# Moving the preparation of the next batch to other steps in a two-stage DFT and gated feed-forward kernel

## The chip, the cores and the metric

One core of a Trainium2 chip. The time is device time in microseconds of one execution, the median of repeated runs; smaller is better. The engines named below are TensorE (PE), VectorE (DVE), ScalarE (ACT), GpSimd (POOL) and SyncE (SP), which here only issues DMAs. Each engine works through its own instructions in the order in which the program lists them.

## The reference

For x of shape 8 x 3008 x 256 (batch, sequence, channel) the real part of a two-dimensional Fourier transform is taken over sequence and channel, and each of the 24064 resulting rows goes through a feed-forward block with the gate h cos h:

```python
X = np.fft.fft(x, axis=1)
X = np.fft.fft(X, axis=2)
a = X.real.astype(np.float32)            # 8 x 3008 x 256
h = a.reshape(-1, 256) @ w_in            # 24064 x 2048
g = h * np.cos(h)
out = (g @ w_out).astype(np.float32)     # 24064 x 256
```

## The kernel before

The channel transform is folded into w_in once at the start (WC and WS, line 351). The sequence transform of length 3008 = 47 x 64 is done per batch in two stages on PE. For x of a batch:

- `load_x` (line 139) brings one of four pieces p into a tile xp (four buffers): six DMAs for piece 0, four for the others, all on SP.
- `fold` (line 210) makes sums and differences of channel halves into xf (one buffer). In batches after the first that is one POOL operation for each of e = 0 and 1 (line 218); e = 1 adds a small ACT copy of two channels (line 225).
- `first_half` (line 231) multiplies a chunk c of xf by a 94-row DFT matrix into a PSUM tile pz (lines 241 to 251) and ACT copies it out (line 260). In batches after the first pz has the tag "fft", which has one buffer.
- `store_z` and `load_z` (lines 266, 278) pass the result through DRAM to change its layout, by SP DMAs.
- `second_half` (line 290) does the second stage of one group g of output rows: four matmuls into a PSUM tile pb, tag "fft" too (line 297), an ACT copy into pq (line 313), and two SP DMAs, one behind the other, that spread one row of pq over 128 partitions as nb (lines 319, 320).

The feed-forward part is a hand-written software pipeline. A batch has six groups (width 225 for group 0, else 256), each with eight steps of 256 hidden units, 48 steps in a batch and 384 in all. The main loop runs over t (line 740). A step `cur` at time t does `mm1(cur, 0)`, PE matmuls with WC into H; `act_e`, which copies twice H to ew (line 464); `mm1(cur, 1)`, matmuls with WS into the same H, which must wait until ew has been read; `dve_h` (line 469), the second side of the symmetric pair; and two ACT roundings (line 484). The gate follows over the next two values of t: `dve_frac` (488), `act_sin` (494), `dve_g` (498), `dve_s` (509 to 518). `mm2` of the step three earlier (line 545) accumulates seven products into M. `seed` (line 429) has ACT write the initial value of the next step's H from nb.

After the last step of a group, ACT copies M out (`take_m`, line 566), POOL combines (`combine_m`, lines 584 to 594; this runs in the steps with t mod 8 = 2 to 4), and `store_out` (line 634) transposes half of the result on DVE (line 637) into ob, then issues the output DMAs on SP (line 647), eight for each half of an ordinary group.

`transform(b)` (line 330) lists, by step of the batch before, the calls that prepare batch b: loads, folds, first stage, intermediate store and load, second stage. The main loop calls what is listed for a step at the end of that step, after `store_out` (line 786) and after the opening's own calls (line 790). The order in the program is the order of each engine's queue: what is called later stands behind what was called before on SP, POOL, ACT, DVE and PE alike.

Of the kernel before, what the change touches and what calls it, by code (L numbers as in the profile page):

```python
# [26 lines left out]
NG = 6  # L27
LAG = 3
# [64 lines left out]
def _runs(g, sg):  # L93


    runs = []
    for j, n, c in _cols(g):
        a, k = c, 0
        if sg:
            a, j = 256 - c - n, (N2 - j) % N2  # L100
            if j == 0:
                a, k, n = a + 1, 33, 31
        runs.append((a // 32, j, k, n))
    return runs
# [3 lines left out]
def kernel(  # L108
# [8 lines left out]
    NB = x.shape[0]  # L117
# [205 lines left out]
    def spread_nb():  # L323
        pq, nb = ready[0, 0]
        T = _width(0)
        pn = psum("pn", "M")
        nc.tensor.matmul(pn[:, 0:T], lhsT=ones, rhs=pq[0:1, T : 2 * T], start=True, stop=True)
        nc.scalar.copy(out=nb[:, 0:T], in_=pn[:, 0:T])

    def transform(b):  # L330
        todo = {}

        def at(o, *call):
            todo.setdefault(o, []).append(call)

        for p in range(4):
            at(8 * p + (0 if p else 3), load_x, b, p)
            for c, o, f in ((2 * p, 6, 8), (2 * p + 1, 9, 13)):
                at(8 * p + o, fold, b, c, 0)
                at(8 * p + o, fold, b, c, 1)  # L340
                at(8 * p + f, first_half, b, c)
                at(8 * p + f + 1, store_z, b, c)
        at(23, load_z, b, 0)
        at(39, load_z, b, 1)
        for g in range(NG):
            at(42 + g, second_half, b, g)
        return todo

    def fold_weights(e, n, tag="M"):
        W = WS if e else WC
        pw = psum("pw", tag)
        for i in range(2):
            nc.tensor.matmul(  # L355
                pw,
                lhsT=CS[i][:, 128 * e : 128 * e + 128],
                rhs=wr[n // 2][i][:, 512 * (n % 2) : 512 * (n % 2) + 512],
                start=(i == 0),
                stop=(i == 1),  # L360
            )
        nc.scalar.copy(out=W[:, 512 * n : 512 * n + 512], in_=pw)
# [74 lines left out]
    def seed_first(s):  # L437
        for u in range(2):
            nc.tensor.matmul(
                s.H[:, u * s.T : u * s.T + s.T],  # L440
                lhsT=wrow[:, 128 * u : 128 * u + 128],
                rhs=s.pq[0:1, s.T : 2 * s.T],
                start=False,
                stop=True,
                skip_group_check=True,
            )

    def mm1(s, e):
        T = s.T
        W = WS if e else WC  # L450
        for u in range(2):
            f = 2 * s.fp + u
            nc.tensor.matmul(  # L453
                s.H[:, u * T : u * T + T],
                lhsT=W[:, 128 * f : 128 * f + 128],
                rhs=s.pq[:, e * T : e * T + T],
                start=False,
                stop=True,
                skip_group_check=True,
            )  # L460

    def act_e(s):
        s.ew = spool.tile([128, 512], FP, tag="ew", bufs=2, name="ew")
        nc.scalar.mul(out=s.ew[:, 0 : 2 * s.T], in_=s.H[:, 0 : 2 * s.T], mul=2.0)  # L464
# [21 lines left out]
    def dve_frac(s, sg):  # L486
        r, h = side(s, sg)
        nc.vector.scalar_tensor_tensor(  # L488
            out=r, in0=r, scalar=-BIG, in1=h, op0=ALU.add, op1=ALU.subtract
        )  # L490
# [5 lines left out]
    def dve_g(s, sg):  # L496
        r, h = side(s, sg)
        nc.vector.scalar_tensor_tensor(  # L498
            out=r, in0=h, scalar=-0.25, in1=r, op0=ALU.add, op1=ALU.mult
        )  # L500
# [57 lines left out]
    def take_m(s, part):  # L558
        T = s.T
        key = (s.b, s.grp)  # L560
        if part == 0:
            mrs[key] = spool.tile([128, 7 * 256], FP, tag="mr", bufs=1, name="mr")
        mv = mrs[key].rearrange("p (m t) -> p m t", m=7)[:, :, 0:T]
        for k in (2, 3) if part else (0, 1):
            n = 1 if k == 3 else 2
            nc.scalar.mul(
                out=mv[:, 2 * k : 2 * k + n],
                in_=acc[key][k].rearrange("p (m t) -> p m t", m=2)[:, 0:n, 0:T],
                mul=TWO_PI,
            )  # L570
# [26 lines left out]
    def combine_last(s):  # L597
        key = (s.b, s.grp)
        M5, M3 = acc[key][2], acc[key][3]
        mv = mrs.pop(key).rearrange("p (m t) -> p m t", m=7)  # L600
        outs[key] = spool.tile([128, 7 * 256], FP, tag="cb", bufs=1, name="cb")
        cv = outs[key].rearrange("p (m t) -> p m t", m=7)
        tt, stt = nc.vector.tensor_tensor, nc.vector.scalar_tensor_tensor
        more = dict(op0=ALU.mult, op1=ALU.add)
        tt(out=cv[:, 0], in0=mv[:, 0], in1=mv[:, 1], op=ALU.add)
        stt(out=cv[:, 4], in0=M5[:, 256:512], scalar=-TWO_PI, in1=mv[:, 0], **more)
        stt(out=cv[:, 6], in0=M5[:, 0:256], scalar=TWO_PI, in1=cv[:, 4], **more)
        stt(out=cv[:, 1], in0=M3[:, 0:256], scalar=TWO_PI, in1=cv[:, 6], **more)
        store_last(s, 0)
        tt(out=cv[:, 5], in0=cv[:, 4], in1=mv[:, 3], op=ALU.add)  # L610
        tt(out=cv[:, 2], in0=cv[:, 5], in1=mv[:, 2], op=ALU.add)
        stt(out=cv[:, 3], in0=M5[:, 0:256], scalar=TWO_PI, in1=cv[:, 5], **more)
        store_last(s, 1)
# [20 lines left out]
    def store_out(s, sg):  # L634
        ob = spool.tile([128, 512], FP, tag="ob", bufs=2, name="ob")
        ov = ob.rearrange("p (t c) -> p t c", c=64)
        nc.vector.transpose(
            out=ov.rearrange("p t (c j) -> p j t c", j=2),
            in_=outs[s.b, s.grp][:, 512 * sg : 512 * sg + 512],
        )  # L640
        for t0, j, k, n in _runs(s.grp, sg):
            to = out_r[s.b, j].rearrange("k (q c) -> q k c", c=64)
            for i in range(0, n, 32):
                m = min(32, n - i)
                src, dst = ov[:, t0 + i // 32], to[:, k + i : k + i + m]
                if m == 32:
                    nc.sync.dma_start(out=dst, in_=src)  # L647
                    continue
                for q in range(4):
                    nc.sync.dma_start(out=dst[q], in_=src[32 * q : 32 * q + m])  # L650
# [70 lines left out]
    for b in range(NB):  # L721
        for g in range(NG):
            for fp in range(8):
                s = Step()
                s.b, s.grp, s.fp, s.T = b, g, fp, _width(g)
                steps.append(s)
    per = NG * 8
    n = len(steps)

    def step(t, last=None):  # L730
        s = steps[t] if 0 <= t < n else None
        return s if s is not None and (last is None or s.fp == 7) else None
# [7 lines left out]
    for t in range(n + LAG + 1):  # L740
        cur, prev, old, done = step(t), step(t - 1), step(t - 2), step(t - LAG)
        if cur:
            if t % per == 0:
                todo = transform(cur.b + 1) if cur.b + 1 < NB else {}
            mm1(cur, 0)
            if t == 0:
                seed_first(cur)
            act_e(cur)
            if t == 0:
                spread_nb()  # L750
                fold_weights(1, 3)
        if t - LAG - 1 == n - 1:
            combine_last(steps[n - 1])
            break
        if step(t - LAG - 1, True):
            take_m(step(t - LAG - 1), 1)
            combine_m(step(t - LAG - 1))
        if done:
            mm2(done, 0)
        if old:  # L760
            dve_g(old, 0)
            dve_g(old, 1)
        if step(t + 1):
            seed(step(t + 1))
        if prev:
            dve_frac(prev, 0)
        if old:
            dve_s(old, 0)
        if prev:
            dve_frac(prev, 1)  # L770
            act_sin(prev)
        if old:
            dve_s(old, 1)
        if step(t - LAG, True):
            take_m(done, 0)
        if cur:
            mm1(cur, 1)
        if done:
            mm2(done, 1)
        if cur:  # L780
            dve_h(cur)
            act_round(cur, 0)
            act_round(cur, 1)
        if old:
            dve_s(old, 2)
        if step(t - LAG - 2, True):
            store_out(step(t - LAG - 2), 0)
        if step(t - LAG - 3, True):
            store_out(step(t - LAG - 3), 1)
        for call in opening.pop(t, ()):  # L790
            call[0](*call[1:])
        for call in todo.pop(t % per, ()):
            call[0](*call[1:])


# [28 lines left out]
```

## Time and profile before

| what | us |
|---|---|
| median of 3 runs (1974.46 to 1974.85) | 1974.66 |
| span of the profiled execution | 1973.1 |
| first step of the main loop starts | 38.4 |
| batch 0, first step to first step of batch 1 | 247.1 |
| each of batches 1 to 6 | 241.1 |
| batch 7, first step to end of span | 241.0 |
| PE / DVE / ACT / POOL busy | 1948.9 / 1854.4 / 1482.7 / 465.1 |
| POOL waiting in `fold` for PE to release xf (line 218 on line 251) | 547.9 |
| SP waiting for the DVE before an output DMA (line 647) | 841.0 |

The span is that of one execution, from its first to its last instruction. A row of the timeline gives a start in us from the start of the span, a length, the engine and line, the operation with its output and inputs, and how many like instructions it merges; a bracket at its end gives idle time of the engine just before and what ended it. A row of busy time by stretch gives the stretch, its length, busy us and number of instructions of PE, weight loads, DVE, ACT and POOL, the granted TensorE clock, the DMA share and GB/s. Rows of neighbouring matmuls overlap, since they are pipelined; the distance from start to start is their cost. The letter q behind an engine's name is its sequencer, here the issue of DMAs.

### The profile page before, as it was taken

Reading aid. Unit: us, or ns where it says so; the run is one execution under the profiler, and the core shown is the slowest. Engines: PE = TensorE matmul, PEld = TensorE weight load, DVE = VectorE, ACT = ScalarE, POOL = GpSimd, SP = SyncE. Lnnn points to the kernel's source line nnn. Section 1 sums busy time; section 2 is a strip of 40 time slices with the busy share of each in tenths; the row PEclk is TensorE's granted clock in tenths of the full one; section 3 lists DMA queues with packets and bytes.
Section 4 is the critical chain, followed back from the end, with each engine's and each line's share of the span. In section 5 each row is a group of like instructions: output and inputs, shape, how many; then the busy total and the mean of one; then the engine's idle time right before and its main releaser. Section 6 shows DMA issues by size and latency. Waiting matters only on the chain.

```text
span 1973.1 us, 28657 instructions
## 1 busy us (share of the span) xinstructions
PE 1948.9 (99%) x9360; PEld 1702.4 (86%) x9360; DVE 1854.4 (94%) x3209; ACT 1482.7 (75%) x2687; POOL 465.1 (24%) x428
## 2 busy tenths in 40 slices
PE   8999999999999999999999999999999999999998
PEld 4888899888988889888898888988889888898887
DVE  2999989999899998999989999999999999899998
ACT  3777777777777777777877777777777777778775
POOL 1123113221133212223222322123311233112111
PEclk9999999999999999999999999999999999999999
DMA  8413221131212212122122301223022220200000
GB/s 194 100 41 62 41 43 31 40 59 35 43 33 46 51 36 43 38 59 38 34 41 51 63 20 37 45 53 55 19 42 53 43 51 21 47 21 10 19 15 22
DMA packets 176682, 88.63 MB, mean 45 GB/s; under 512 B 103303, under 2 KB 173622, under 8 KB 174902
## 3 DMA queue, kind: packets, MB, share of 16 engines
q1 hardware_dynamic: 176374, 86.68, 21.4%
q8 instruction: 75, 1.23, 0.3%
q14 instruction: 73, 0.60, 0.1%
q10 hardware_dynamic: 160, 0.13, 0.0%
HBM read 49.50 MB, written 37.27 MB: 44 GB/s over the span
## 4 chain that ended last, share of the span: by engine, by line
PE 91%; DVE 5%; DMA 2%; ACT 1%; issue 1%; SPq 0%; DVEq 0%; POOL 0%; ACTq 0%; POOLq 0%
PE M L545 53%; PE H L453 31%; PE pz L244 3%; PE pb L297 2%; DVE r L498 1%; DMA xp<-in_x_dram 1%; DVE S L516 1%; DVE S L509 1%; DVE S L518 1%; DVE h L469 1%; DVE r L488 1%; ACT r L484 0%; PE pw L355 0%; DMA out_dram<-ob 0%; SPq L647 0%
## 5 line engine op out<-in xcount | busy, mean ns | idle before, releaser
L494 ACT ACTIVATE r<-r 128x1024 f32<-128x1024 f32 (+1 forms) x384 | 398.5, 1038 | 303.6 <-DVE r L488 302.7
L545 PE MATMUL M<-S,VX 128*128 128x256 f32 (+1 forms) x2304 | 612.3, 375 | 0.0
L545 PEld LDWEIGHTS M<-S,VX 128*128 128x128 f32 x2304 | 437.8, 190 | 49.9
L453 PE MATMUL H<-pq,WS 128*128 128x256 f32 (+1 forms) x1536 | 390.2, 376 | 11.5 <-ACT ew L464 11.2
L453 PE MATMUL H<-pq,WC 128*128 128x256 f32 (+1 forms) x1536 | 393.9, 379 | 0.5 <-ACT H L429 0.5
L545 PE MATMUL M<-r,w 128*128 128x256 f32 (+1 forms) x1536 | 387.7, 375 | 0.0
L429 ACT ACTIVATE H<-nb,wn 128x256 f32<-128x256 f32 (+1 forms) x766 | 362.9, 474 | 18.0 <-DVE r L498 5.6
L469 DVE TENSOR_TENSOR h<-ew,H 128x512 f32<-128x512 f32 (+1 forms) x384 | 256.8, 669 | 92.5 <-PE H L453 86.5
L453 PEld LDWEIGHTS H<-pq,WS 128*128 128x128 f32 x1536 | 289.3, 190 | 53.9 <-ACT ew L464 20.0
L545 PEld LDWEIGHTS M<-r,w 128*128 128x128 f32 x1536 | 300.7, 197 | 27.0
L488 DVE SCALAR_TENSOR_TENSOR r<-r,h 128x512 f32<-128x512 f32 (+1 forms) x384 | 309.5, 806 | 0.0
L453 PEld LDWEIGHTS H<-pq,WC 128*128 128x128 f32 x1536 | 283.2, 190 | 28.9 <-ACT H L429 0.8
L218 POOL TENSOR_TENSOR xf<-xp 94x508 f32<-94x508 f32 x112 | 165.4, 1497 | 566.0 <-PE pz L251 547.9
L509 DVE TENSOR_TENSOR S<-r 128x512 f32<-128x512 f32 (+1 forms) x384 | 290.2, 756 | 0.1
L498 DVE SCALAR_TENSOR_TENSOR r<-h,r 128x512 f32<-128x512 f32 (+1 forms) x384 | 272.6, 710 | 0.0
L484 ACT ACTIVATE r<-H 128x512 f32<-128x512 f32 (+1 forms) x384 | 222.9, 580 | 55.7 <-DVE h L469 52.7
L464 ACT ACTIVATE ew<-H 128x512 f32<-128x512 f32 (+1 forms) x384 | 225.4, 587 | 50.3 <-PE H L453 43.8
L488 DVE SCALAR_TENSOR_TENSOR r<-r,H 128x512 f32<-128x512 f32 (+1 forms) x384 | 255.1, 664 | 0.0
L498 DVE SCALAR_TENSOR_TENSOR r<-H,r 128x512 f32<-128x512 f32 (+1 forms) x384 | 254.0, 661 | 0.3 <-ACT r L494 0.3
L484 ACT ACTIVATE r<-h 128x512 f32<-128x512 f32 (+1 forms) x384 | 236.2, 615 | 0.0
L545 PE MATMUL M<-S,w 128*128 128x256 f32 (+1 forms) x768 | 225.2, 375 | 0.0
L545 PE MATMUL M<-r,VX 128*128 128x256 f32 (+1 forms) x768 | 225.1, 375 | 0.0
(72 smaller groups left out, 1498.4 us busy)
## 6 DMA issues: line engine op xcount, KB each, us to landing
out_dram<-ob SPq DMA_DIRECT2D x728, 32.0 KB
xp<-in_x_dram SPq DMA_DIRECT2D x56, 256.0 KB
zd<-zs SPq DMA_DIRECT2D x112, 96.0 KB
z<-zd SPq DMA_DIRECT2D x28, 384.0 KB
xp<-in_x_dram SPq DMA_DIRECT2D x56, 120.0 KB
nb<-nd SPq DMA_DIRECT2D x40, 128.0 KB
wr<-in_moe_w_in_dram SPq DMA_DIRECT2D x8, 256.0 KB
w<-in_moe_w_out_dram SPq DMA_DIRECT2D x4, 512.0 KB
```

Of the source, the lines that this page charges most:

```text
L218: (nc.gpsimd if b else nc.vector).tensor_tensor(out=fv[:, e, :, 1:128], in0=xv[:, :, 1:128], in1=xv[:, :, 255:128:-1], op=ALU.subtract if ...
L244: nc.tensor.matmul(pz[rows, a:512], lhsT=w, rhs=fv[:, e, a:512], start=True, stop=True)
L429: nc.scalar.activation(out=s.H[:, u * T : u * T + T], in_=s.nb[:, 0:T], func=AF.Copy, bias=0.25, scale=wn[:, f : f + 1],)
L453: nc.tensor.matmul(s.H[:, u * T : u * T + T], lhsT=W[:, 128 * f : 128 * f + 128], rhs=s.pq[:, e * T : e * T + T], start=False, stop=True, ...
L464: nc.scalar.mul(out=s.ew[:, 0 : 2 * s.T], in_=s.H[:, 0 : 2 * s.T], mul=2.0)
L469: nc.vector.tensor_tensor(out=s.h[:, 0 : 2 * T].rearrange("p (u t) -> p u t", u=2)[:, :, ::-1], in0=s.ew[:, 0 : 2 * T].rearrange("p (u t) ...
L484: nc.scalar.activation(out=r, in_=h, func=AF.Copy, bias=BIG, scale=1.0)
L488: nc.vector.scalar_tensor_tensor(out=r, in0=r, scalar=-BIG, in1=h, op0=ALU.add, op1=ALU.subtract)
L494: nc.scalar.activation(out=r, in_=r, func=AF.Sin, bias=0.0, scale=SIN_SCALE)
L498: nc.vector.scalar_tensor_tensor(out=r, in0=h, scalar=-0.25, in1=r, op0=ALU.add, op1=ALU.mult)
L509: nc.vector.tensor_tensor(out=sv[:, 0:2], in0=gv[:, 2:3].to_broadcast([128, 2, T]), in1=gv[:, 0:4:3], op=ALU.subtract,)
L545: nc.tensor.matmul(acc[key][m // 2][:, 256 * (m % 2) : 256 * (m % 2) + T], lhsT=w, rhs=a, start=first, stop=s.fp == 7, skip_group_check=True,)
```

## The change

The dictionary of preparing calls is now one for the whole run, keyed by the absolute step, and filled before the main loop for batches 1 to 7, so that a call can be put into a step beyond the 48 of the batch before. Step numbers of the calls change, and the two `store_out` calls of a group come one step later.

```diff
+    todo = {}
+    per = NG * 8
+
     def transform(b):
-        todo = {}
-
         def at(o, *call):
-            todo.setdefault(o, []).append(call)
+            todo.setdefault(per * (b - 1) + o, []).append(call)
 
         for p in range(4):
-            at(8 * p + (0 if p else 3), load_x, b, p)
-            for c, o, f in ((2 * p, 6, 8), (2 * p + 1, 9, 13)):
+            at(8 * p + (1 if p else 5), load_x, b, p)
+            for c, o, f in ((2 * p, 7, 9), (2 * p + 1, 9, 15)):
                 at(8 * p + o, fold, b, c, 0)
                 at(8 * p + o, fold, b, c, 1)
                 at(8 * p + f, first_half, b, c)
                 at(8 * p + f + 1, store_z, b, c)
-        at(23, load_z, b, 0)
-        at(39, load_z, b, 1)
-        for g in range(NG):
-            at(42 + g, second_half, b, g)
-        return todo
+        at(25, load_z, b, 0)
+        at(41, load_z, b, 1)
+        for g, o in enumerate((44, 46, 49, 51, 54, 57)):
+            at(o, second_half, b, g)
...
     n = len(steps)
+    for b in range(1, NB):
+        transform(b)
...
-            if t % per == 0:
-                todo = transform(cur.b + 1) if cur.b + 1 < NB else {}
...
-        if step(t - LAG - 2, True):
-            store_out(step(t - LAG - 2), 0)
         if step(t - LAG - 3, True):
-            store_out(step(t - LAG - 3), 1)
+            store_out(step(t - LAG - 3), 0)
+        if step(t - LAG - 4, True):
+            store_out(step(t - LAG - 4), 1)
         for call in opening.pop(t, ()):
             call[0](*call[1:])
-        for call in todo.pop(t % per, ()):
+        for call in todo.pop(t, ()):
             call[0](*call[1:])
```

By step of the batch, before and after:

| call | before | after |
|---|---|---|
| load of x, piece 0 / piece p | 3 / 8p | 5 / 8p + 1 |
| fold of chunks 2p and 2p + 1 | 8p + 6, 8p + 9 | 8p + 7, 8p + 9 |
| first stage of chunks 2p and 2p + 1 | 8p + 8, 8p + 13 | 8p + 9, 8p + 15 |
| loads of the intermediate result | 23, 39 | 25, 41 |
| second stage of groups 0 to 5 | 42 to 47 | 44, 46, and 1, 3, 6, 9 of the next batch |
| transposes and output DMAs, t mod 8 | 4, 5 | 5, 6 |

## The prediction, made before the changed kernel was run

> **What bounds the kernel now.** I read the page first, then busy time by stretch, then the timeline engine by engine in batch 4 and the first group of batch 7. "Step" is the loop's t counted within a batch (0 to 47).
>
> ```profile
> PE 1948.9 (99%) x9360; PEld 1702.4 (86%) x9360; DVE 1854.4 (94%) x3209; ACT 1482.7 (75%) x2687; POOL 465.1 (24%) x428
> PE 91%; DVE 5%; DMA 2%; ACT 1%; issue 1%; SPq 0%; DVEq 0%; POOL 0%; ACTq 0%; POOLq 0%
> ```
>
> TensorE is busy nearly always, and the chain of waits is 91% PE. The change alters no matmul, so it can win only where PE waits now, and lose where it makes PE wait. The DVE's 5% says where to look.
>
> ```profile
> 1008.78:1045.36 36.58, 35.37 (x178) 33.28 (x177) 34.53 (x64) 27.07 (x52) 9.17 (x8) 1.00 0.25 47
> 1732.06:1766.93 34.87, 34.87 (x179) 33.36 (x178) 32.81 (x64) 26.75 (x51) 6.42 (x8) 1.00 0.09 22
> ```
>
> These are steps 0 to 7 (group 0, width 225) of batch 4 and of batch 7, which prepares no successor: length, then busy time of PE, weight loads, DVE, ACT, POOL. Unstalled, these steps take 3 x 4.54 + 5 x 4.18 = 34.5 us (first matmuls of the steps of batch 7: 1732.06, 1736.60, 1741.14, 1745.68, 1749.87, 1754.06). So PE loses 2.04 us here in batch 4, 0.33 in batch 7. Batches 1 to 6 repeat this within 0.02 us. Every later step stands at its matmuls' own length (4.75 plain, 5.92 with a first-stage call, 5.64 with a second-stage call), so this is all there is to win inside a batch.
>
> ```profile
> 1029.92 3.02 POOL L218 TENSOR_TENSOR xf<-xp 94x508 f32<-94x508 f32 x2
> 1030.37 1.45 DVE L516 TENSOR_TENSOR S<-S,r 128x225 f32<-128x225 f32 x1
> 1036.39 0.38 DVE L516 TENSOR_TENSOR S<-S,r 128x225 f32<-128x225 f32 x1
> 1033.88 1.03 PE L453 MATMUL H<-pq,WS 128*128 128x225 f32 x4 [0.65 <-ACT ew L464]
> 1038.84 1.03 PE L453 MATMUL H<-pq,WS 128*128 128x225 f32 x4 [0.50 <-ACT ew L464]
> ```
>
> A DVE operation with both inputs in SBUF takes 1.45 us instead of 0.38 while a fold runs on POOL. The fold, loaded early, runs straight behind the combine. From h (line 469) to h the DVE needs 3.82 us in a free width-225 step, 5.98 in step 3 (4.91 in batch 7, with the combine and no fold), and 4.41 with a transpose; PE needs 4.18. In batch 4 h stands 1.94 us behind the WS matmuls in step 4, and the next WS matmuls come 0.82 late; then 1.78 and 0.66. Both times 1.12 us of lag cost nothing.
>
> **The change, part by part.** (1) Second-stage calls of groups 2, 3 and 4 now fall in steps 1, 3 and 6 of group 0. Each adds 0.89 us of PE (5.64 against 4.75). The transposes go from steps 4 and 5 to 5 and 6, the fold leaves. DVE against PE: step 3 4.91 to 5.07, step 4 3.82 to 4.18, step 5 4.41 to 4.18, step 6 4.41 to 5.07. The lag never passes 0.34, well under 1.12, and the stall goes: 6 x 2.04 + 0.33 = **-12.6 us**. PE's own total is the same, as steps 42 to 47 lose what the others gain. If this cover failed, the 12.6 stays.
>
> (2) The first x load of a batch moves from step 3 to step 5, and on SP's queue that is behind the output DMAs of the same step, which wait for the DVE transpose.
>
> ```profile
> 1011.11 0.38 SPq L146 DMA_DIRECT2D xp<-in_x_dram  x1
> 1033.84 9.76 SPq L647 DMA_DIRECT2D out_dram<-ob  x16
> 1043.70 0.42 SPq L146 DMA_DIRECT2D xp<-in_x_dram  x1
> 1042.66 0.19 ACT L225 COPY xf<-xp 94x8 f32<-94x8 f32 x1
> 1042.76 0.54 ACT L464 ACTIVATE ew<-H 128x450 f32<-128x450 f32 x1
> ```
>
> Today x is asked for at 1011.11 and read on ACT at 1042.66, by line 225, with ew queued right behind it. After, with step 5 starting at 0: WS at 2.28, its end and h at 3.31, then h 0.53, line 518 0.30, transpose 0.70: done at 4.84. Eight output DMAs hold SP for 5.1 (half of the sixteen, with their gaps): first x DMA at 10.0. Six-DMA loads land, by the semaphores of the trace, 7.5 to 8.0 us after their first issue on an idle queue; four-DMA loads behind output DMAs 6.2 to 6.7. I take 7.2, nearer the same number of DMAs: x is there at 17.2 (16.2 to 18.0). Line 225's turn comes 1.57 after h of step 7: 4.18 + 5.07 + 3.31 + 1.57 = 14.1. So ACT stands still for 3.1 us, with ew of step 8, the seeds, and sin behind it. Step 8 starts at 13.43 and its WS matmuls could start 2.38 later, at 15.81; they need ew, which now starts at 17.35 and takes 0.59, and 0.05 more: 17.99. **PE stalls 2.2 us** (1.2 to 3.0) in each of batches 1 to 6: **+13.2**. Later loads, folds and intermediate transfers keep leads of about six steps (28 us) or the same distances as now; nothing for them.
>
> (3) In step 9 of batches 1 to 6 two calls meet: second stage of group 5, then first stage of the next batch. Both use tag "fft", one PSUM buffer, so the second must wait for ACT's copy of the first. Now they never share a step.
>
> ```profile
> 1003.14 1.03 PE L453 MATMUL H<-pq,WC 128*128 128x256 f32 x4
> 1003.34 0.59 ACT L313 COPY pq<-pb 128x512 f32<-128x512 f32 x1 [0.28 <-PE pb L297]
> ```
>
> PE runs on at 1003.14 behind the second-stage matmuls; the copy starts 0.20 later, takes 0.59, and 0.05 passes until PE sees it: 0.84 us at least. An ACT held up by a DVE lag of 1.08, as step 12 shows, makes it 1.8 at most. I expect the lag to be small behind the stall of (2): 0.9, 6 x 0.9 = **+5.4**.
>
> (4) Batch 0 loses 0.82 in step 7 (5.00 against 4.18) and 0.95 in step 8 (6.64 against 5.69). Without the fold in step 5 the DVE saves 1.40 there (1.82 against 0.76 on line 419, 0.72 against 0.38 on line 518) and about 0.3 of stall remains. But its x load now follows the nb DMA that ends at 69.5, lands near 77, and the fold falls into step 8, without the first-stage matmuls that covered it: two operations stretched as at 1051.45 (line 509, 1.58 for 0.62) and 1052.96 (line 488, 1.75 for 0.68) bring some 1.0 back. **-0.5** (-1.8 to +1.5).
>
> Those rows never stretch one operation by more than 1.07 us under a POOL operation of 1.5. The Trainium skill (SBUF — State Buffer, "SBUF: two separate sides") calls the shared port an exclusive lock held for the whole instruction. By that, two fold operations could hold the DVE for 3.0 us instead of 2.0, and batch 0 would end at +0.6; the trace fits it only in part.
>
> (5) Groups 1 to 4: folds and transposes shift by a step or two. Lag there reaches 1.0 to 1.2 of a tolerance near 1.5 (width 256 gives ew 0.4 us more); I take nothing.
>
> Sum: -12.6 + 13.2 + 5.4 - 0.5 = +5.5 us on a span of 1973.1. The median of the runs lies 1.6 us above that span, taken as the same after: 1974.7 + 5.5 = **1980.2 us**. Own range, with the bounds of (2) to (4) not all at one end at once: 1973 to 1987.
>
> **Rivals.** *x in time (faster).* If DMAs behind the transposes go out and land so fast that x is there by 15.1, (2) is zero: 1974.7 - 12.6 - 0.5 + 5.4 = 1967. It needs 10.3 us from transpose to landing; the quickest rows add to 5.1 + 6.2 = 11.3. 0.13.
>
> *DVE becomes the bound in groups 1 to 4.* Both folds might stretch by 1.9 (steps 16 and 24 do, steps 13, 21 and 29 only 0.7 to 1.0). Then 8 x 4.36 + 1.0 for transposes + 1.5 for the combine + 3.8 = 41.2 against PE's 40.5: 0.7 us in 28 groups, +19.6, 1999.8. Against it: larger lag makes the stretch smaller. 0.08.
>
> *The clock falls.* At the end the granted clock goes to 0.50 at 1970.35, 2.7 us after the last matmul ended (1967.66); a 1.4 us gap at 51 us left it at 1.00. A stall of (2) near its 3.0 could do that; one step of 4.39 at half clock costs 4.4 more, six times 26: 2007. 0.06. The Trainium skill (TensorE: Matmul & The Clock Gate, "What's actually happening") puts the fall after an idle window of about 3.4 us, longer than my stall; with that window at half speed the price would be an estimated 1.7 us each, about 1990.
>
> *The stall of group 0 stays* because PE's added work doesn't meet the lag: 1980.2 + 12.6 = 1992.8. 0.05.
>
> **How the numbers follow.** Forecast 0.66, rivals 0.13, 0.08, 0.06, 0.05, 0.02 for the rest. 0.2% is 3.9 us, about what a measurement tells from no change: the forecast's +5.5 has some 0.36 of its chance below that line. Faster 0.15, same 0.24, slower 0.61. Range 1966 to 1987: it takes in the faster rival and leaves out the three dear ones.
>
> **What would show it.** Step 5 to 7 of group 0 at 4.18, 5.07, 4.18; ACT idle about 3 us before line 225 on x in step 7, and WS of step 8 waiting for ew; POOL's fold waiting for x; in step 9 a PE gap of 0.9 on ACT's pq copy. No ACT wait for x would make it wrong on the fast side; DVE without idle time in groups 1 to 4 on the slow side.

## The result and the profile after

The changed kernel takes 1982.37 us (median of 5 runs, 1982.19 to 1983.23) against 1974.66 us: +7.7 us, a ratio of 1.0041 (95% interval 1.0028 to 1.0053). It is slower by more than 0.2%. The profiled execution has a span of 1980.6 us, 7.5 more than before.

From the page of the changed kernel, busy time of the engines and the chain that ended last, by engine:

```profile
PE 1950.7 (98%) x9360; PEld 1700.4 (86%) x9360; DVE 1862.7 (94%) x3209; ACT 1474.7 (74%) x2687; POOL 457.4 (23%) x428
...
PE 89%; DVE 3%; DMA 2%; ACT 2%; SPq 2%; issue 1%; POOL 0%; DVEq 0%; ACTq 0%
```

The DVE's part of the chain fell from 5% to 3%, but SP and ACT, which had 0% and 1%, now have 2% each. The stall that was aimed at went, and others came. The page shows no more than that; busy time by stretch shows where (columns as before; the first two rows are steps 0 to 7 of batches 4 and 7, then steps 8, 9 and 12 of batch 4):

```profile
1008.06:1045.39 37.33, 37.33 (x201) 36.12 (x200) 34.71 (x67) 29.60 (x56) 5.79 (x6) 1.00 0.16 38
1735.39:1772.73 37.34, 37.34 (x201) 36.11 (x200) 34.71 (x67) 29.61 (x56) 6.04 (x8) 1.00 0.10 24
1045.39:1050.96 5.57, 4.66 (x23) 4.10 (x23) 3.91 (x9) 3.36 (x8) 2.60 (x2) 1.00 0.37 72
1050.96:1058.38 7.42, 6.65 (x44) 5.90 (x43) 7.13 (x14) 5.16 (x9) 0.00 (x0) 1.00 0.07 18
1067.62:1073.16 5.54, 5.02 (x24) 4.14 (x23) 5.54 (x10) 3.59 (x7) 2.14 (x3) 1.00 0.00 0
```

Group 0 now holds three second-stage calls, 34.5 + 3 x 0.89 = 37.2 us of PE work, and takes 37.33: PE is busy throughout. Steps 8, 9 and 12 are longer than their work (4.39, 6.58 and 4.75). With the step starts of both traces (first WC matmul to first WC matmul, less the same step's length where nothing stalls it), the whole difference can be booked:

| where PE stalls | before, us | after, us | difference | forecast |
|---|---|---|---|---|
| group 0, steps 4 to 7, batches 1 to 7 | 12.4 | 0.7 | -11.7 | -12.6 |
| step 8, batches 1 to 6 | 0 | 8.3 | +8.3 | +13.2 |
| step 9, batches 1 to 6 (0.83 each) | 0 | 5.0 | +5.0 | +5.4 |
| step 12, batches 1 to 7 (0.79 each) | 0 | 5.5 | +5.5 | 0 |
| steps 13, 21, 29, 37 (0.03 to 0.07 each) | 0 | 1.5 | +1.5 | 0 |
| batch 0, steps 7 to 9 | 1.8 | 1.6 | -0.2 | -0.5 |
| before the first step | 38.4 | 37.5 | -0.9 | 0 |
| sum | | | +7.5 | +5.5 |

The first step of the main loop starts between 36.6 and 38.4 us in the ten traces of this document, whatever was edited, so the -0.9 ahead of it is not put down to the change.

The two stalls that were foreseen look like this in the timeline of batch 4 (start, length, engine, line, operation, count):

```profile
1036.83 4.63 SPq L647 DMA_DIRECT2D out_dram<-ob  x8
1041.59 0.39 SPq L146 DMA_DIRECT2D xp<-in_x_dram  x1
...
1048.10 0.21 ACT L225 COPY xf<-xp 94x8 f32<-94x8 f32 x1 [1.91 <-DMA out_dram<-ob]
1048.21 0.59 ACT L464 ACTIVATE ew<-H 128x512 f32<-128x512 f32 x1
1048.85 1.13 PE L453 MATMUL H<-pq,WS 128*128 128x256 f32 x4 [0.91 <-ACT ew L464]
...
1055.36 1.05 PE L297 MATMUL pb<-BJ,z 128*128 128x128 f32 x8
1057.17 0.45 PE L241 MATMUL pz<-xf,L 94*64 94x128 f32 x4 [0.77 <-ACT pq L313]
```

SP issues eight output DMAs, then the x load. ACT stands idle for 1.91 us before line 225, ew follows, and PE's WS matmuls of step 8 wait for ew. The bracket names an output DMA, but line 225 reads only x; the semaphores of the six x DMAs rise until 1047.92, 0.18 before it starts, so the label is a wrong guess among events of the same moment. In step 9 the first-stage matmuls wait for ACT's copy of the second-stage result.

The stall that was not foreseen is on the DVE. In batch 7, from the timeline of before and then of after: two successive h (line 469, steps 10 and 11), and between them the start of the combine's second operation on POOL (line 585).

```profile
1779.23 0.69 DVE L469 TENSOR_TENSOR h<-ew,H 128x512 f32<-128x512 f32 x1
1782.79 1.18 POOL L585 TENSOR_TENSOR cb<-mr 128x225 f32<-128x225 f32 x1 [1.69 <-ACT mr L566]
1784.17 0.67 DVE L469 TENSOR_TENSOR h<-ew,H 128x512 f32<-128x512 f32 x1
```

```profile
1785.93 0.69 DVE L469 TENSOR_TENSOR h<-ew,H 128x512 f32<-128x512 f32 x1 [0.96 <-ACT r L494]
...
1788.98 0.67 POOL L585 TENSOR_TENSOR cb<-mr 128x225 f32<-128x225 f32 x1 [1.88 <-ACT mr L566]
1789.72 1.47 POOL L586 TENSOR_TENSOR cb<-cb,mr 128x450 f32<-128x450 f32 x1
1790.11 1.62 DVE L488 SCALAR_TENSOR_TENSOR r<-r,h 128x512 f32<-128x512 f32 x1
1792.46 0.68 DVE L469 TENSOR_TENSOR h<-ew,H 128x512 f32<-128x512 f32 x1
1794.83 1.13 PE L453 MATMUL H<-pq,WS 128*128 128x256 f32 x4 [0.52 <-ACT ew L464]
```

Before, line 585 starts 3.56 us after h and the DVE's round from h to h is 4.94 us (3.71 and 5.09 in batches 1 to 6). After, it starts 3.05 us after h and the round is 6.53: four of the DVE's two-input operations are stretched (lines 518, 509, 488 and 516) instead of two (498 and 516). The lag (how far h stands behind the end of its WS matmuls) is then 2.04 us at step 11, and ew, with it the WS matmuls of step 12, come late: the step loses 0.79, so 1.25 us of lag cost nothing here.

### The profile page after: what moved, and what is told of

It reads as the page before. It is cut to its first block, busy times and chain, and to the rows that moved or that the text cites. A ratio compares the mean times of both kernels' runs of the same rounds, so it can differ in the third digit from the quotient of the medians.

```text
span 1980.6 us, 28675 instructions
## 1 busy us (share of the span) xinstructions
PE 1950.7 (98%) x9360; PEld 1700.4 (86%) x9360; DVE 1862.7 (94%) x3209; ACT 1474.7 (74%) x2687; POOL 457.4 (23%) x428
## 4 chain that ended last, share of the span: by engine, by line
PE 89%; DVE 3%; DMA 2%; ACT 2%; SPq 2%; issue 1%; POOL 0%; DVEq 0%; ACTq 0%
PE M L545 52%; PE H L453 31%; PE pz L244 3%; PE pb L297 2%; DMA xp<-in_x_dram 2%; SPq L647 1%; DVE r L498 1%; ACT ew L464 1%; DVE h L469 1%; DVE S L509 1%; ACT r L484 0%; ACT r L494 0%; DVE S L518 0%; PE pw L355 0%; DVE S L516 0%
## 5 line engine op out<-in xcount | busy, mean ns | idle before, releaser
L218 POOL TENSOR_TENSOR xf<-xp 94x508 f32<-94x508 f32 x112 | 159.3, 1442 | 724.8 <-PE pz L251 576.2
L498 DVE SCALAR_TENSOR_TENSOR r<-h,r 128x512 f32<-128x512 f32 (+1 forms) x384 | 286.0, 745 | 0.0
L509 DVE TENSOR_TENSOR S<-r 128x512 f32<-128x512 f32 (+1 forms) x384 | 285.5, 744 | 0.1
```

What stands on the lines that cost most here:

```text
L218: (nc.gpsimd if b else nc.vector).tensor_tensor(out=fv[:, e, :, 1:128], in0=xv[:, :, 1:128], in1=xv[:, :, 255:128:-1], op=ALU.subtract if ...
L498: nc.vector.scalar_tensor_tensor(out=r, in0=h, scalar=-0.25, in1=r, op0=ALU.add, op1=ALU.mult)
L509: nc.vector.tensor_tensor(out=sv[:, 0:2], in0=gv[:, 2:3].to_broadcast([128, 2, T]), in1=gv[:, 0:4:3], op=ALU.subtract,)
```

## The experiments

Eight kernels, in two groups. The kernel before, run beside each group, had medians of 1974.54 and 1974.55. The changed kernel was not run again; its 1982.37 stands beside 1974.66.

**x load in step 4.**

```diff
-            at(8 * p + (1 if p else 5), load_x, b, p)
+            at(8 * p + (1 if p else 4), load_x, b, p)
```

> The changed kernel with the first x load of a batch called in step 4 instead of 5, so that on SP's queue it stands ahead of the output DMAs that wait for the DVE transpose. Theory (ACT waits for x in step 7): x lands in step 6, the ACT wait and the 1.1 to 1.8 us stall of step 8 vanish in batches 1 to 6, some 0.4 us comes back because the fold then runs beside the transposes of step 6: 0.8 us a batch, 4 to 7 us faster than the changed kernel, 1975.5 to 1978.5. Rival (the stall of step 8 comes from the DVE lag or the fold, not from x): no change, 1982.

Measured 1978.02 (ratio to before 1.0016, interval 1.0006 to 1.0025), 4.3 below the changed kernel. From its timeline, batch 4:

```profile
1030.72 0.38 SPq L146 DMA_DIRECT2D xp<-in_x_dram  x1
...
1036.58 11.01 SPq L647 DMA_DIRECT2D out_dram<-ob  x16
```

The load now stands ahead of all sixteen output DMAs, and ACT doesn't wait for x in any batch. Stalls of step 8 fall from 8.3 to 0.4 us, group 0 takes back 2.2 (the fold runs beside the transposes, 1.07 us in step 7 of batches 1 and 3, 0.34 in step 8 of batch 4, nothing in batches 2, 5 and 6), and batch 0 loses 1.1 more, 0.4 of it by a fall of the clock (last section). That x was late on ACT is shown: the position of one DMA call in SP's queue was worth about 8 us in step 8, of which the run as a whole keeps 4.3.

**Group 5 in step 12, and in step 11.**

```diff
-        for g, o in enumerate((44, 46, 49, 51, 54, 57)):
+        for g, o in enumerate((44, 46, 49, 51, 54, 60)):
```

> The changed kernel with the second-stage call of group 5 in step 12 of the next batch instead of step 9, so that it never shares a step with a first-stage call. Theory (one PSUM buffer shared): the 0.83 us of step 9 vanish in six batches, 5 us faster, near 1977.4; the 0.8 us stall of step 12 stays in batches 1 to 6, where the first-stage call still lengthens step 9, and goes in batch 7, where nothing lengthens it any more: another 0.8. Rival for the stall of step 12 (POOL's fold right ahead of the combine): it stays in batches 1 to 6 too but batch 7, which has no fold, is not changed by this edit. Rival for step 9 (the first-stage matmuls wait for their fold): nothing changes in step 9, 1982.

The second kernel has 59 in place of 60:

> As the run with group 5 in step 12, but in step 11, where 0.89 us of added PE work lies between the late h of step 11 and the matmuls of step 12 that wait for it. Theory (a DVE lag of 2.0 us at step 11 against a tolerance of about 1.4): the stall of step 12 is covered in all seven batches, 0.8 us each: 5 us below the run with step 12 and 10 us below the changed kernel, near 1972.5. Rival (the stall of step 12 is not a matter of lag): same time as the run with step 12.

Measured 1974.06 and 1974.08 (ratios 0.9999, 0.9989 to 1.0008, and 0.9998, 0.9989 to 1.0007): the same as before, and 8.3 below the changed kernel where I expected 5.8 and 10. In the timeline of the first, step 9 of batch 4 has its first-stage matmuls without any wait:

```profile
1050.57 1.03 PE L453 MATMUL H<-pq,WS 128*128 128x256 f32 x4
1052.67 0.45 PE L241 MATMUL pz<-xf,L 94*64 94x128 f32 x4
```

So the shared PSUM buffer is the cause in step 9: 5.0 us gone. The stall of step 12 went too, in all seven batches, with 0.25 left in step 11 of batches 1 to 6. That refutes both of my explanations for it. A first-stage call still lengthens step 9 in batches 1 to 6, and the fold still runs just ahead of the combine, yet there is no stall. And since it had already gone, the cover that step 11 was to give had nothing to cover: no difference between the two kernels, and no test of the cover.

**Both edits.**

> Both edits: x load in step 4 and group 5 in step 11. If the three losses are separate they add: 10 + 5 us below the changed kernel, near 1967, below the kernel before too. If the x load and the collision share their time (one hides the other), less: 1970 to 1972.

Measured 1968.99 (0.9973, 0.9963 to 0.9984): 13.4 below the changed kernel and below the kernel before. The two parts add (4.3 + 8.3 = 12.6); I had counted on 2 us more from a cover that wasn't needed.

**The spread of second-stage calls alone**, in the kernel before: the new call table of the change with its six steps 44 to 57, all else as before.

> The kernel before with the second-stage calls alone moved (steps 44, 46, and 1, 3, 6, 9 of the next batch); loads, folds, first stage and transposes as before. In group 0 the fold still runs behind the combine, so part of the stall stays: lag 1.05 after step 3, 1.8 after step 4, some 0.95 us of stall against 2.04, 7 us gained in all. Against that, step 9 is lengthened by its second-stage call as in the changed kernel, and if the stall of step 12 comes from that length alone, it appears in all seven batches here too: +5.5. Together near 1973. Rival (the stall of step 12 needs the collision with the first-stage call): 1968. Rival (the spread alone brings the whole 12.6): 1962.

Measured 1974.15 (0.9999, 0.9990 to 1.0009). Group 0 loses 4.4 instead of 12.4 us, and step 12 loses 0.79 in all seven batches, although no first-stage call is in step 9. So the stall of step 12 needs neither the collision nor the fold (batch 7 has none); a second-stage call in step 9, beside those in steps 1, 3 and 6, suffices. Over all ten traces, in batches 1 to 7, it goes with one number, the distance from h of step 10 to line 585: 3.05 us in the changed kernel, in the runs with the x load in step 4 and with the transposes put back (below), and here, with a DVE round of 6.53; 3.56 to 3.72 in the other six, with 4.94 to 5.09.

**The transposes alone**, in the kernel before: the two calls of `store_out` one step later.

> The kernel before with the transposes and output DMAs alone one step later. The DVE's work over steps 3 to 7 of group 0 stays the same, so its stall stays near 2 us and only moves by a step: 1974.7, within 1 us. Rival (it is the transposes' place that takes the stall of group 0 away): 8 to 12 us faster. Rival (the later output DMAs alone delay loads): slower by some us.

Measured 1970.70 (0.9982, 0.9972 to 0.9991): 3.9 below the kernel before, where I expected nothing. From its timeline:

```profile
1030.39 1.03 PE L453 MATMUL H<-pq,WS 128*128 128x225 f32 x4 [0.65 <-ACT ew L464]
1032.60 0.61 DVE L469 TENSOR_TENSOR h<-ew,H 128x450 f32<-128x450 f32 x1
1034.75 1.03 PE L453 MATMUL H<-pq,WS 128*128 128x225 f32 x4
```

The DVE does the same work in steps 3 to 7, but about 1.0 us of lag costs a step of group 0 nothing (the prediction's 1.12 comes from how late the WS matmuls start; the steps lose 0.1 more than that). With the transpose out of step 4, h of step 5 lies 1.18 us behind the WS matmuls instead of 1.78; step 6 loses 0.18 instead of 0.77, and batch 7 nothing. Group 0 goes from 12.4 to 8.6 us. With the 8.0 of the spread that makes 11.8, the 11.7 that the whole change wins there; the third part of the change in group 0, the later fold, was not run alone.

**The transposes put back**, in the changed kernel.

> The changed kernel with the transposes and output DMAs alone put back one step earlier. The x load of step 5 then stands behind sixteen output DMAs, the last eight of which wait for the transpose of step 5: first issue about 10.4 us after the start of step 5 instead of 9.7, so 0.7 more stall in step 8 of six batches, 4 us slower than the changed kernel: 1985 to 1988. Rival (the later transposes are what costs): 1976 to 1979.

Measured 1994.48 (1.0104, 1.0089 to 1.0119), 12 above the changed kernel; the direction was right, the size not. ACT's wait for x grows as expected: in batch 4 SP issues its first x DMA 10.8 us after the start of step 5 instead of 9.65 (10.2 to 10.5 in the other batches), and PE waits 2.20 us for ew.

```profile
1057.22 0.20 ACT L225 COPY xf<-xp 94x8 f32<-94x8 f32 x1 [3.21 <-DMA xp<-in_x_dram]
1057.97 1.13 PE L453 MATMUL H<-pq,WS 128*128 128x256 f32 x4 [2.20 <-ACT ew L464]
```

Step 8 loses 13.7 us in place of 8.3, of which some 1.5 by a fall of the clock (below). Steps 14, 15, 22, 23, 30, 31, 38 and 39 lose 0.12 each in most batches, 6.2 in all. The transposes there follow straight on the combine again, and the lag at steps 13 and 14 is 1.36 us instead of 0.76 and 0.88. So the later transposes are a gain of the change, in group 0 and here.

**Early fold.** Group 5 in step 11, and from batch 2 on:

```diff
-            at(8 * p + (1 if p else 5), load_x, b, p)
-            for c, o, f in ((2 * p, 7, 9), (2 * p + 1, 9, 15)):
+            at(8 * p + 1 if p else 4 if b == 1 else -1, load_x, b, p)
+            for c, o, f in ((2 * p, 1 if p == 0 and b > 1 else 7, 9), (2 * p + 1, 9, 15)):
```

> The version with group 5 in step 11, and from batch 2 on the first x load called in the last step of the batch before that and its first fold in step 1, so that the fold runs on POOL in steps 0 and 1, where the DVE has 0.4 and 1.5 us of idle time. If the 0.3 to 1.1 us still lost in steps 7 and 8 with the load in step 4 is the fold beside the transposes, it goes: 2 to 4 us below that version, 1965 to 1967. Rival (the loss moves with the fold): 1969 or more.

Measured 1966.41 (0.9959, 0.9944 to 0.9974): the fastest of all, 8.1 us below the kernel before. Group 0 and step 8 together lose about 0.5 us in batches 1 to 7 (9.0 in the changed kernel); batch 0, whose steps 7 and 8 still lose 1.1 each, is not helped. In the timeline of batch 4 the fold has ended two us before the combine begins:

```profile
1011.63 2.86 POOL L218 TENSOR_TENSOR xf<-xp 94x508 f32<-94x508 f32 x2 [27.54 <-DMA xp<-in_x_dram]
1016.53 0.73 POOL L584 TENSOR_TENSOR cb<-mr 128x256 f32<-128x256 f32 x1 [2.03 <-ACT mr L566]
```

## Why the prediction was right, and where it was not

The time came out 2.2 us above the forecast, on the forecast side, by the two mechanisms that it named. That it came so near is partly luck: the 4.9 us that part (2) had too much and the 7.0 us that part (5) put at nothing nearly cancel.

- *Part (1), the stall of group 0:* right, -11.7 for -12.6. Its working was not: the lag was to stay under 0.34, and it reaches 1.51 at step 3, since the DVE's round of step 2 takes 5.74 us, not 4.37. The second-stage call behind step 3 takes it up; 0.10 us per batch remains. I had priced the spread and the transposes as one; the two single runs divide it, 8.0 and 3.8.
- *Part (2), x late:* right in mechanism and place, too large in size, 8.3 for 13.2. The first x DMA was issued at 9.65 us after the start of step 5 (forecast 10.0), and ACT's copy of x (line 225) ran 6.3 to 7.2 us after it (forecast 7.2 to the landing, taken nearer the rows with as many DMAs; the rows behind output DMAs, 6.2 to 6.7, were the better guide). ACT waited 1.9 to 2.6 us in place of 3.1.
- *Part (3), the shared PSUM buffer:* right, 0.83 us each, the lower bound from the rows.
- *Part (4), batch 0:* -0.2 for -0.5.
- *Part (5), groups 1 to 4 at nothing:* this step failed, by 7.0 us. I took the combine's contention from the rows of before and checked only whether the sum of lags stayed under the tolerance. The rows held for one phase of POOL against the DVE. The second-stage call that I had in hand for step 9 in part (3) shifts that phase by half a microsecond, and the round costs 1.6 us more. The rival "DVE becomes the bound" had the right engine, but for other work (two folds), in all groups, at 19.6 us; the trace has it in one step of group 1. Of the 7.0, 1.5 are the small stalls behind it and in groups 2 to 4: the lag at steps 20, 28 and 36 of batches 1 to 6 reaches 1.31 us, over the 1.0 to 1.2 forecast, and what costs nothing is 1.25, not near 1.5.

The clock, another rival, stayed at 1.00 through the stalls of step 8 in the changed kernel (1.2 to 1.9 us each). In the kernel with the transposes put back it fell once there, and cost about 1.5 us instead of 4.4 (last section).

What makes a second-stage call in step 9 bring the combine forward is only partly shown. The traces show that ACT's sin of the step (line 494) then no longer waits for the DVE (0.61 us in step 10 of batch 7 before, none after) and that the copies of M stand right behind it. In batches 1 to 7 the sin of step 10 waits 0 us in the four kernels with the stall of step 12, and 0.61 to 1.12 us in the other six. A first-stage call lengthens step 9 too, but behind it the fold holds up the DVE, and the sin waits 1.11 us (run with step 12).

The early fold shows the same in group 0. With a second-stage call in step 1 the sin of step 2 waits 0 instead of 0.31 us, and the round that begins there takes 5.75 instead of 4.37. With the early fold that call is still in step 1, but the DVE is held up, the sin waits 0.96 to 1.35 us in batches 1 to 6, and the round takes 4.90. Line 585 starts 3.10 us after h in step 2 both where the round takes 4.37 and where it takes 5.75, so that distance alone does not set the round. No run changes the wait of the sin alone.

## What to carry to other kernels

Where a DMA call is moved on a queue that other calls wait on, count what stands ahead of it and what those calls wait for: here eight output DMAs behind a transpose made a load late that had 24 us to spare. A call that is moved takes its PSUM buffer with it, so list which calls now share a step and a buffer. A lag below the tolerance is free and above it is paid in full, so equal work in another step is not equal time.

## What the runs showed of the hardware

*Contention depends on phase.* In the changed kernel the DVE's line 488 starts at 1790.11, POOL's line 586 ends at 1791.19, and the DVE operation ends at 1791.73, 0.54 us later; alone the same operation takes 0.68. In batch 4 of the kernel before, the fold's first operation ended at 1031.57 and line 516, begun at 1030.37, at 1031.82; the second ended at 1032.94 and line 518 at 1033.19. So the DVE waits for the end of the POOL operation in progress, as the Trainium skill says (SBUF — State Buffer, "SBUF: two separate sides": whichever of the two starts first has the pair for the whole instruction); I had called the agreement partial. It holds for every such operation of the changed kernel: the 155 of lines 488, 498 and 509 at width 256 that begin at least 0.15 us before a POOL operation of the fold or the combine ends all end 0.54 or 0.55 us after it. What an operation loses is thus what is left of the POOL operation when it starts, less some 0.13 us, and in batch 7 half a microsecond of shift between the DVE and the combine's six operations changes a round by 1.6 us.

*The clock falls after gaps shorter than I had taken.* In the kernel with the transposes put back, PE waits 1.95 us in batch 2, and soon after the granted clock is 0.50; columns as before, with the clock behind POOL's figure (the last two rows are from batch 4):

```profile
565.22:568.63 3.41, 1.46 (x8) 1.06 (x7) 1.25 (x3) 1.41 (x4) 1.38 (x2) 1.00 0.22 44
568.60:572.00 3.40, 3.40 (x11) 2.92 (x10) 2.53 (x5) 2.15 (x4) 1.12 (x1) 0.50 0.04 12
572.00:573.00 1.00, 1.00 (x7) 0.93 (x6) 1.00 (x3) 0.21 (x1) 0.00 (x0) 0.98 0.00 0
1053.33:1056.74 3.41, 2.43 (x13) 1.98 (x11) 2.92 (x6) 0.68 (x2) 0.00 (x0) 1.00 0.64 132
1056.74:1060.15 3.41, 2.18 (x11) 2.08 (x12) 0.94 (x3) 2.64 (x6) 2.48 (x2) 1.00 0.12 38
```

It stays at 0.50 for 3.41 us and costs about 1.5 us (step 8 loses 3.58 in this batch, 1.75 to 2.48 in the others). A gap of 2.20 us in batch 4 of the same trace left it at 1.00, so it is not the gap's length alone that decides. Three of the ten traces show the same fall in the opening, near 52 us, behind gaps of 0.64, 1.44 and 0.46 us; traces that keep 1.00 there have the same three gaps.

What decides can be worked out from the ten traces. Counted from the moment at which the granted clock first reaches 1.00 (5.43 us in this trace), every fall comes after a whole number of stretches of 3.413 us; the one at 568.63 comes after 165. The stretch just before it has 1.46 us of PE work (first row), while the gap of batch 4 is split between two stretches with 2.43 and 2.18 us (last rows). In all ten traces PE is busy for at most 1.63 us in the stretch before a fall, those in the opening and at the end included, and for at least 1.68 us in every other stretch at full clock. So where a gap lies on this grid counts as well as its length. The Trainium skill (TensorE: Matmul & The Clock Gate, "What's actually happening") gives 3.413 us and a window that runs freely: both agree; that a whole idle window is needed does not agree, since the stretch at 565.22 has 1.46 us of PE work.
